# Slot sums of experts 0 to 3 over all 512 columns at once, and where the output tokens stand among the slot sums

## The chip, the core and the metric

The kernel runs on one core of a Trainium2 chip. The metric is the device time of one execution in microseconds (us). A core has a matrix engine (TensorE, PE in the profile, with its weight loads as PEld), a vector engine (VectorE, DVE), a scalar engine (ScalarE, ACT), GpSimd (POOL) and a sync engine (SyncE, SP) that in this kernel issues nearly all of the DMAs. Matrix products land in PSUM, and DVE or ACT copies them from there to SBUF.

## What is computed

```python
attn_out = _attn_ref(q, k, v)                       # windowed attention, 4 x 8 x 576 x 64
x = attn_out.transpose(0, 2, 1, 3).reshape(2304, 512)
x = (x @ w_a * (x @ w_b)) @ w_out                   # gated product, d_ff 1536
logits = x @ phi                                    # 2304 x 32: 8 experts, 4 slots each
d = softmax(logits, axis=0); c = softmax(logits, axis=1)
slot_input = (d.T @ x).reshape(8, 4, 512)
for e in range(8):
    slot_out[e] = maximum(slot_input[e] @ w1[e], 0) @ w2[e]   # w1: 512x1024, w2: 1024x512
out = c @ slot_out.reshape(32, 512)                 # 2304 x 512
```

All inputs and outputs are float32. The change touches only the last two lines: the product with `w2`, here called the slot sums, and the product with `c`, here called the tokens.

## The kernel before

Up to about 457 us the kernel works through attention, the gated product and the logits. Then come the eight experts, in two units: unit `u` = 0 has experts 0 to 3, unit 1 has experts 4 to 7. The slots of four experts lie side by side in the matrix engine, 32 columns each, so four matmuls (one for each expert) make one group.

- **Weights.** `w1` and `w2` come by DMA, on SP's queue, through a list of places in SBUF (`fetch`, `source`, line 782). The order of the loads is fixed: `w1`; then `w2` of experts 0 to 3 over all 512 columns, then of experts 4 and 5 over all 512 columns (keys `"r"`); then `w2` of experts 6 and 7 in halves of 256 columns (keys `"c"`), the left halves of both experts first and the right halves last. A place is loaded again when the products that read it are done. The last load is issued before the first output is.
- **Slot sums** (`slots_out`, line 1022). For a half `n` of the 512 columns and a unit `u`, eight groups (`m` = 0 to 7) of four matmuls of 256 columns add into one PSUM tile `ops`. The trace shows two records for each of these float32 matmuls.
- **Choice of slots** (`pick`, line 1029). DVE copies `ops` to SBUF as `o` (line 1072), and four small matmuls with the selection matrix `sel` add both units' slots into `so`.
- **`split`** (lines 1035 and 1036) copies `so` to `sor` on ACT and then subtracts on DVE; the tokens read `sor`.
- **Tokens** (`tokens_out`). For one of nine pairs of token tiles `j` and a half `n`: two matmuls into a PSUM bank `op` (line 1048; four banks take turns), a copy to SBUF `ob` (line 1053) by ACT when the running number is even and by DVE when it is odd, and one DMA of 256 KB to the output (line 1054) on SP's queue. There are 18 of these: nine for the left half, nine for the right.

In the last block (from line 1057) the order on PE is written by hand. It is: left half, unit 0, unit 1; choice; right half, unit 0, where the left half's tokens begin behind `m` = 4; right half, unit 1, with the other left tokens behind `m` = 0 to 4; choice; the nine right tokens. The order on DVE and ACT in this block comes from a scheduler, in before; each engine then works in the order it was given.

Of the kernel before, what the change touches and what calls it, by code (L numbers as in the profile page):

```python
# [11 lines left out]
F32 = mybir.dt.float32  # L12
# [9 lines left out]
P = 128  # L22
# [32 lines left out]
MANUAL = {mybir.EngineType.PE}  # L55
# [9 lines left out]
def swa_glu_softmoe_kernel(  # L65
# [13 lines left out]
    nc = tc.nc  # L79
    B, H, S, D = q.shape  # L80
    NT, DM = out.shape
# [4 lines left out]
    NTILE = NT // P  # L86
# [5 lines left out]
    MF = F2 // P  # L92
# [5 lines left out]
    N_EX1 = 4  # L98
    N_EX2 = 6
    WHOLE = 6  # L100
    EARLY = 4
    HALF = DM // 2

    dram = ctx.enter_context(tc.tile_pool(name="dram", bufs=1, space=bass.MemoryType.DRAM))
# [4 lines left out]
    p2 = ctx.enter_context(tc.tile_pool(name="p2", bufs=2))  # L109
# [3 lines left out]
    pools = {}  # L113

    ps_ab = ctx.enter_context(tc.tile_pool(name="ps_ab", bufs=1, space=PSUM))
    ps_s = ctx.enter_context(tc.tile_pool(name="ps_s", bufs=1, space=PSUM))
# [670 lines left out]
    def use(key):  # L787
        used.add(key)
        return exw[key]
# [32 lines left out]
    for t in range(NFIRST, NTILE):  # L822
        s = sA[t]
# [12 lines left out]
    for t in range(NTILE):  # L836
        if t < NTILE - NLAST:
            r = R[t]
# [7 lines left out]
            if t + 1 in beside:  # L846
                p = R[t + 1] - r
                o = (1, 2, 3) if p == 3 else (p / 3, 2 * p / 3, p)
            else:
                o = (1, 2.5, 3)  # L850
# [10 lines left out]
    a, b, c = LAST  # L861
# [83 lines left out]
    with tc.manual_schedule(engines=MANUAL | {mybir.EngineType.Activation, mybir.EngineType.DVE}):  # L945
# [8 lines left out]
        for m in range(MJ):  # L954
            for j in range(4):
                f = MJ * j + m
# [9 lines left out]
        for h in range(2):  # L966
            c = slice(DM // 2 * h, DM // 2 * (h + 1))
# [46 lines left out]
    def w2(e, m, n):  # L1014
        h, c = m // 4, m % 4
        if e >= WHOLE:
            return use(("c", (n, h, e), c))
        return (use if n else exw.get)(("r", (h, e), c))[:, HALF * n:HALF * n + HALF]

    def slots_out(op, u, m, n):  # L1020
        for e in range(4):
            nc.tensor.matmul(  # L1022
                op[32 * e:32 * e + 32], lhsT=hTs[u][m // 4][:, m % 4, 32 * e:32 * e + 32], rhs=w2(4 * u + e, m, n),
                start=(m == 0), stop=(m == MF - 1),
            )

    def pick(so, u, o):

        nc.tensor.matmul(
            so, lhsT=exs["sel"][:, u].rearrange("p a s -> p (a s)"), rhs=o, start=(u == 0), stop=(u == 1)  # L1030
        )

    def split(so):
        sor = exs["ex2"].tile([P, HALF], F32R, tag="as0", name="sor", bufs=2)
        nc.scalar.copy(out=sor, in_=so)
        nc.vector.tensor_tensor(out=sor[W:P], in0=so[W:P], in1=sor[W:P].bitcast(F32), op=ALU.subtract)
        return sor
# [5 lines left out]
    def tokens_out(n, j, sor):  # L1043
        i = j + NTILE // 2 * n
        pool, tag = banks[i % 4]
        op = pool.tile([P, 2, HALF], F32, tag=tag, name="op")
        for k in range(2):
            nc.tensor.matmul(op[:, k], lhsT=cts[2 * j + k], rhs=sor)  # L1048
        if i % 4 == 0:
            tag = ("w2", "w2", "w1", "w1", "w3")[i // 4]  # L1050
            obs[0] = wp.tile([P, 4, 2, HALF], F32, tag=tag, name="ob", bufs=wbufs[tag])
        ob = obs[0][:, i % 4]
        evac[i % 2](out=ob, in_=op)
        nc.sync.dma_start(
            out=out[2 * P * j:2 * P * (j + 1), HALF * n:HALF * (n + 1)].rearrange("(i p) d -> p i d", p=P), in_=ob
        )

    with tc.manual_schedule(engines=MANUAL):
        for n in range(2):
            os = {}  # L1060
            so = (ps_m, ps_t)[n].tile([P, HALF], F32, tag="mx"[n], name="so", bufs=1)
            for u in range(2):
                op = ps_s.tile([P, HALF], F32, tag=f"s{u}", name="ops")
                for m in range(MF):
                    slots_out(op, u, m, n)
                    if n and u and m < NTILE // 2 - EARLY:
                        tokens_out(0, EARLY + m, sor)
                    if n and not u and m >= MF - EARLY:
                        tokens_out(0, m - MF + EARLY, sor)
                for c in range(0, HALF, P):  # L1070
                    os[u, c] = p2.tile([P, P], F32, tag="l4", name="o", bufs=3)
                    nc.vector.tensor_copy(os[u, c], op[:, c:c + P])
                    for v in range(2 if u else 0):
                        pick(so[:, c:c + P], v, os[v, c])
            sor = split(so)
        for j in range(NTILE // 2):
            tokens_out(1, j, sor)


# [28 lines left out]
```

## Time and profile before

| | us |
|---|---|
| time, median of 3 runs (523.2 to 524.25) | 523.6 |
| the profiled execution | 524.17 |
| its span, first to last instruction | 522.4 |
| PE busy in the span | 489.7 (94%) |
| DVE, ACT, POOL busy | 297.6, 193.7, 65.5 |
| DMA moved | 116.51 MB, mean 223 GB/s |

The profiled execution is 524.17 - 522.4 = 1.77 us longer than its span. The busy shares are means over stages that have different limits. The change lies in the last 45 us of the span, and this stretch has three parts: weights arrive while the slot sums are formed (to 496 us), PE works without a gap of note (to 511 us), and the output drains (to 522.4 us). Times below are counted from the start of the span.

### The profile page before, as it was taken

Reading aid. Unit: us, or ns where it says so; the run is one execution under the profiler, and the core shown is the slowest. Engines: PE = TensorE matmul, PEld = TensorE weight load, DVE = VectorE, ACT = ScalarE, POOL = GpSimd, SP = SyncE. Lnnn points to the kernel's source line nnn. Section 1 sums busy time; section 2 is a strip of 40 time slices with the busy share of each in tenths; the row PEclk is TensorE's granted clock in tenths of the full one; section 3 lists DMA queues with packets and bytes.
Section 4 is the critical chain, followed back from the end, with each engine's and each line's share of the span. In section 5 each row is a group of like instructions: output and inputs, shape, how many; then the busy total and the mean of one; then the engine's idle time right before and its main releaser. Section 6 shows DMA issues by size and latency. Waiting matters only on the chain.

```text
span 522.4 us, 10689 instructions
## 1 busy us (share of the span) xinstructions
PE 489.7 (94%) x4047; PEld 361.7 (69%) x4047; DVE 297.6 (57%) x753; ACT 193.7 (37%) x586; POOL 65.5 (13%) x136
## 2 busy tenths in 40 slices
PE   5769999899999999999999999999999999999593
PEld 3547787678778787777777778787787777534252
DVE  3998898689146757647574755676833210512033
ACT  4786766544214423324232432343422112330022
POOL 4100100000000112120311112123331000100000
PEclk9798999999999999999999999999999999999798
DMA  9999965642136877678786776787799999799956
GB/s 254 271 274 295 311 166 203 220 142 80 42 77 155 205 203 202 187 177 206 202 199 173 157 187 166 175 217 187 197 246 315 337 356 335 263 404 396 355 180 204
DMA packets 135043, 116.51 MB, mean 223 GB/s; under 512 B 81744, under 2 KB 111952, under 8 KB 134992
## 3 DMA queue, kind: packets, MB, share of 16 engines
q1 hardware_dynamic: 130256, 101.15, 67.3%
q0 software_dynamic: 4736, 14.68, 9.6%
q8 instruction: 32, 0.52, 0.4%
q14 instruction: 19, 0.16, 0.1%
HBM read 91.16 MB, written 24.64 MB: 222 GB/s over the span
## 4 chain that ended last, share of the span: by engine, by line
PE 77%; DMA 11%; DVE 7%; ACT 2%; issue 1%; SPq 0%; DVEq 0%
PE psb L455 27%; PE psa L455 25%; DMA xw<-in_moe_w_dram 6%; PE xps L365 3%; DMA wo_dram<-wo 3%; PE s L274 3%; PE ups L633 3%; PE ops L1022 3%; PE ups L530 2%; PE tk L139 1%; PE op L1048 1%; PE tg L139 1%; PE tq L139 1%; PE tp L139 1%; PE two L139 1%
## 5 line engine op out<-in xcount | busy, mean ns | idle before, releaser
L455 PE MATMUL psb<-wb,x 128*128 128x512 f32 x648 | 167.1, 400 | 1.8 <-DVE g L467 1.4
L455 PE MATMUL psa<-wa,x 128*128 128x512 f32 x648 | 167.5, 400 | 0.0
L455 PEld LDWEIGHTS psb<-wb,x 128*128 128x128 f32 x648 | 117.4, 188 | 29.1 <-issue 2.8
L455 PEld LDWEIGHTS psa<-wa,x 128*128 128x128 f32 x648 | 117.5, 188 | 26.5 <-issue 3.2
L467 DVE TENSOR_TENSOR g<-psb,g 128x512 f32<-128x512 f32 (+1 forms) x54 | 36.6, 679 | 69.8 <-PE psb L455 61.6
L462 ACT COPY g<-psa 128x512 f32<-128x512 f32 x53 | 30.9, 583 | 84.0 <-PE psa L455 79.9
L294 ACT ACTIVATE pr<-pr,nmx 128x128 f32<-128x128 f32 x96 | 37.2, 389 | 17.6 <-DVE nmx L287 17.6
L331 POOL DMA_DIRECT2D pd<-pq x44 | 24.2, 559 | 101.7 <-DVE pq L324 72.6
L503 DVE STREAM_TRANSPOSE gq<-g 128x512 f32<-128x512 f32 x42 | 29.4, 703 | 0.7
L368 ACT CAST x<-xps 128x512 fp32r<-128x512 f32 x18 | 10.5, 585 | 47.5 <-PE xps L365 47.5
L1022 PE MATMUL ops<-xw,hT 128*32 128x256 f32 x256 | 19.9, 414 | 5.6 <-DMA xw<-in_moe_w_dram 5.6
L315 DVE TENSOR_TENSOR pr<-pr,rs 128x512 f32<-128x512 f32 x36 | 24.6, 689 | 1.0
L274 PE MATMUL s<-kTs,qTs 64*64 64x128 f32 x576 | 22.0, 294 | 0.0
L337 POOL DMA_DIRECT2D pT<-pd x22 | 16.5, 755 | 42.3 <-DMA pd<-pq 38.1
L274 PEld LDWEIGHTS s<-kTs,qTs 64*64 64x64 f32 x576 | 17.1, 144 | 5.9 <-issue 4.5
L237 POOL COPY kTs<-kTs 128x256 f32<-128x256 f32 x17 | 8.6, 503 | 97.6 <-DVE kTs L248 65.3
L139 PE MATMUL tq<-ident,ldq 128*128 128x128 f32 x72 | 12.4, 300 | 9.0 <-DMA ldq<-in_q_dram 7.6
L229 ACT ACTIVATE qTs<-tq 128x512 f32<-128x512 f32 x18 | 10.8, 599 | 26.5 <-PE tq L139 26.5
L287 DVE CUSTOM_DVE_ANT_0 pr<-s,masks 128x128 f32<-128x128 f32 x80 | 17.5, 284 | 3.1 <-PE s L274 3.1
L566 ACT ACTIVATE e<-lt,nm 128x128 f32<-128x128 f32 x17 | 6.2, 365 | 34.1 <-DVE nm L562 33.9
L294 ACT ACTIVATE pr<-s,nmx 128x128 f32<-128x128 f32 x48 | 17.0, 376 | 2.8 <-DVE nmx L284 2.8
L294 ACT ACTIVATION_READ_ACCUMULATOR pr<-pr,nmx 128x1 f32 x96 | 17.9, 187 | 0.0
(151 smaller groups left out, 612.5 us busy)
## 6 DMA issues: line engine op xcount, KB each, us to landing
xw<-in_moe_w_dram SPq DMA_DIRECT2D x42, 512.0 KB, 7.0
gd<-gq SPq DMA_DIRECT2D x168, 64.0 KB, 3.0
gT<-gd SPq DMA_DIRECT2D x42, 256.0 KB, 3.3
xw<-in_moe_w_dram SPq DMA_DIRECT2D x26, 256.0 KB, 7.9
st<-in_moe_w_b_dram SPq DMA_DIRECT2D x12, 512.0 KB, 5.7
st<-in_moe_w_out_dram SPq DMA_DIRECT2D x12, 512.0 KB, 5.2
st<-in_moe_w_a_dram SPq DMA_DIRECT2D x12, 512.0 KB, 7.0
pd<-pq POOLq DMA_DIRECT2D x44, 128.0 KB, 3.4
```

The source lines that it names most:

```text
L139: nc.tensor.transpose(o, i, ident)
L274: nc.tensor.matmul(sps[h][c, u], lhsT=qT[r, u, c], rhs=kTs[r, t % 2, u, W * b:W * b + P], start=not early, stop=not early or u == 3,)
L287: nc.vector.tensor_tensor_reduce(out=pr[:, u].rearrange("p (a k) -> p a k", a=2), in0=sps[h][:, u].rearrange("p (a k) -> p a k", a=2), in1 ...
L294: nc.scalar.activation(out=pr[:, u], in_=sps[h][:, u] if early else pr[:, u], func=ACTF.Exp, scale=-1.0, bias=nmx[:, i:i + 1], accum_out=s ...
L315: nc.vector.tensor_tensor(out=pr, in0=pr, in1=rs.to_broadcast([P, 4, P]), op=ALU.mult)
L331: nc.gpsimd.dma_start(out=pd[:, :, i].rearrange("j k e -> k j e"), in_=pq[32 * i:32 * i + 32].rearrange("p j h u q -> p j (h u q)"),)
L337: nc.gpsimd.dma_start(out=pT, in_=pd[:, :, :, P * h:P * h + P].rearrange("j k i e -> (j k) i e"))
L455: nc.tensor.matmul(ps, lhsT=l[:, kk], rhs=r, start=(n == 0), stop=(n == 3 * KD - 1))
L462: nc.scalar.copy(out=pas[t, fg], in_=ps)
L467: nc.vector.tensor_tensor(out=g[:, c:c + step], in0=ps[:, c:c + step], in1=pa[:, c:c + step], op=ALU.mult)
L503: nc.vector.transpose(out=gq.rearrange("p (j c t) -> p c j t", j=4, c=4), in_=gts[t][:, 512 * fg:512 * fg + 512].rearrange("p (c j f) -> p ...
L1022: nc.tensor.matmul(op[32 * e:32 * e + 32], lhsT=hTs[u][m // 4][:, m % 4, 32 * e:32 * e + 32], rhs=w2(4 * u + e, m, n), start=(m == 0), sto ...
```

## The change

The slot sums of unit 0 are formed once, over 512 columns (`slots_out` without `n`), instead of twice over 256; one DVE copy of 512 columns takes the place of four of 128. Unit 1 keeps its two halves. The left half's tokens no longer stand among the groups of the slot sums: five of them (`EARLY` = 5) stand between unit 1's left and right half, and the other four stand behind the choice of the right half, ahead of the nine right tokens. The order on ACT and DVE in this block is now the program's order too.

```diff
-    EARLY = 4
+    EARLY = 5
...
+        if n is None:
+            return use(("r", (h, e), c))
         return (use if n else exw.get)(("r", (h, e), c))[:, HALF * n:HALF * n + HALF]
 
-    def slots_out(op, u, m, n):
+    def slots_out(op, u, m, n=None):
...
-    with tc.manual_schedule(engines=MANUAL):
+    NOUT = NTILE // 2
+    sors = []
+    with tc.manual_schedule(engines=MANUAL | {mybir.EngineType.Activation, mybir.EngineType.DVE}):
+        op = ps_s.tile([P, DM], F32, tag="s0", name="ops")
+        for m in range(MF):
+            slots_out(op, 0, m)
+        o = pools["p3"].tile([P, DM], F32, tag="gT0", name="o", bufs=2)
+        nc.vector.tensor_copy(o, op)
         for n in range(2):
-            os = {}
+            op = ps_s.tile([P, HALF], F32, tag=f"s{1 - n}", name="ops")
+            for m in range(MF):
+                slots_out(op, 1, m, n)
             so = (ps_m, ps_t)[n].tile([P, HALF], F32, tag="mx"[n], name="so", bufs=1)
-            for u in range(2):
-                op = ps_s.tile([P, HALF], F32, tag=f"s{u}", name="ops")
-                for m in range(MF):
-                    slots_out(op, u, m, n)
-                    if n and u and m < NTILE // 2 - EARLY:
-                        tokens_out(0, EARLY + m, sor)
-                    if n and not u and m >= MF - EARLY:
-                        tokens_out(0, m - MF + EARLY, sor)
-                for c in range(0, HALF, P):
-                    os[u, c] = p2.tile([P, P], F32, tag="l4", name="o", bufs=3)
-                    nc.vector.tensor_copy(os[u, c], op[:, c:c + P])
-                    for v in range(2 if u else 0):
-                        pick(so[:, c:c + P], v, os[v, c])
+            for c in range(0, HALF, P):
+                o1 = p2.tile([P, P], F32, tag="l4", name="o", bufs=3)
+                nc.vector.tensor_copy(o1, op[:, c:c + P])
+                pick(so[:, c:c + P], 0, o[:, HALF * n + c:HALF * n + c + P])
+                pick(so[:, c:c + P], 1, o1)
             sor = split(so)
-        for j in range(NTILE // 2):
-            tokens_out(1, j, sor)
+            sors.append(sor)
+            for j in range(EARLY, NOUT) if n else ():
+                tokens_out(0, j, sors[0])
+            for j in range(NOUT if n else EARLY):
+                tokens_out(n, j, sor)
```

On PE, from the last transpose ahead of the slot sums to the end, the order before is this (rows that repeat are cut from the middle; `x63` are 63 matmuls in a row, `ops` are slot sums, `so` is the choice, `op` are tokens at two matmuls each):

```order
L139 MATMUL th<-ident,hs 128x128 x4
L1022 MATMUL ops<-xw,hT 32x256 x63
L1029 MATMUL so<-o,sel 128x128 x4
L1022 MATMUL ops<-xw,hT 32x256 x20
L1048 MATMUL op<-sor,cT 128x256 x2
...
L1022 MATMUL ops<-xw,hT 32x256 x12
L1029 MATMUL so<-o,sel 128x128 x4
L1048 MATMUL op<-sor,cT 128x256 x18
```

and now:

```order
L139 MATMUL th<-ident,hs 128x128 x4
L1024 MATMUL ops<-xw,hT 32x512 x31
L1024 MATMUL ops<-xw,hT 32x256 x32
L1031 MATMUL so<-o,sel 128x128 x4
L1050 MATMUL op<-sor,cT 128x256 x10
L1024 MATMUL ops<-xw,hT 32x256 x32
L1031 MATMUL so<-o,sel 128x128 x4
L1050 MATMUL op<-sor,cT 128x256 x26
```

Between the two choices there stood 64 matmuls of 256 columns and nine tokens; now there are 32 and five tokens, and 13 tokens stand behind the second choice where nine stood. The first 32 matmuls of unit 0 (one of them ahead of the transposes) are 512 columns wide.

On DVE, from the copies of the first slot sums to the end, before:

```order
L1072 COPY o<-ops 128x128 x4
L1036 TENSOR_TENSOR sor<-so,sor 64x256
L1053 COPY ob<-op 128x512
L1072 COPY o<-ops 128x128
L1053 COPY ob<-op 128x512
L1072 COPY o<-ops 128x128
L1053 COPY ob<-op 128x512 x2
L1072 COPY o<-ops 128x128 x2
L1036 TENSOR_TENSOR sor<-so,sor 64x256
L1053 COPY ob<-op 128x512 x5
```

and now:

```order
L1067 COPY o<-ops 128x512
L1075 COPY o<-ops 128x128 x2
L1038 TENSOR_TENSOR sor<-so,sor 64x256
L1055 COPY ob<-op 128x512 x2
L1075 COPY o<-ops 128x128 x2
L1038 TENSOR_TENSOR sor<-so,sor 64x256
L1055 COPY ob<-op 128x512 x7
```

Two output copies stand ahead of the second `sor` and seven behind it, where four and five stood. On ACT it is three and six, where it was five and four.

## Rows read from the trace of the kernel before

**Rows 1.** Chain that ended last: start us, us, what.

```profile
481.88 8.79 DMA xw<-in_moe_w_dram
...
490.71 5.17 PE ops L1022 x58
495.88 1.32 PE so L1029 x8
497.20 2.30 PE ops L1022 x40
...
507.95 1.43 PE ops L1022 x24
509.38 1.36 PE so L1029 x8
...
510.77 0.38 ACT sor L1035
...
511.17 0.44 DVE sor L1036
...
511.66 0.52 PE op L1048 x2
```

**Rows 2.** Timeline, slot sums: start us, us, engine, line, records [idle before <-releaser].

```profile
479.94 4.07 PE L1022 MATMUL ops<-xw,hT 128*32 128x256 f32 x66
488.46 1.06 PE L1022 MATMUL ops<-xw,hT 128*32 128x256 f32 x2 [4.45 <-DMA xw<-in_moe_w_dram]
493.73 1.66 PEld L1022 LDWEIGHTS ops<-xw,hT 128*32 128x32 f32 x26 [0.26 <-DMA xw<-in_moe_w_dram]
```

**Rows 3.** Timeline, unit 0 of the product with w1, 512 columns wide.

```profile
461.98 7.07 PE L989 MATMUL h<-xw,sinT 128*32 128x512 f32 x64 [0.38 <-DVE sinT L980]
```

**Rows 4.** Windows: stretch, its length, busy of each engine; last: PEclk, DMA share, GB/s.

```profile
13.00:14.00 1.00, 0.14 (x2) 0.00 (x0) 0.97 (x2) 1.00 (x5) 0.00 (x0) 1.00 0.99 387
15.00:16.00 1.00, 0.60 (x4) 0.42 (x4) 1.00 (x3) 1.00 (x2) 0.00 (x0) 0.99 0.99 296
16.00:17.00 1.00, 0.44 (x3) 0.45 (x3) 1.00 (x2) 1.00 (x6) 0.47 (x1) 0.50 1.05 324
483.00:484.00 1.00, 1.00 (x14) 0.34 (x6) 0.29 (x2) 0.00 (x0) 0.00 (x0) 1.00 1.05 422
487.00:488.00 1.00, 0.00 (x0) 0.00 (x0) 0.00 (x0) 0.00 (x0) 0.00 (x0) 0.51 1.10 347
490.70:493.80 3.10, 3.09 (x32) 1.45 (x36) 0.00 (x0) 0.00 (x0) 0.00 (x0) 0.50 1.10 348
504.00:505.00 1.00, 1.00 (x14) 0.45 (x14) 0.02 (x1) 0.56 (x1) 0.00 (x0) 1.00 0.66 227
```

**Rows 5.** Timeline, the first left token's copy and the right tokens behind the second choice.

```profile
499.96 0.59 ACT L1053 COPY ob<-op 128x512 f32<-128x512 f32 x1 [2.29 <-PE op L1048]
512.20 3.27 DVE L1053 COPY ob<-op 128x512 f32<-128x512 f32 x5 [0.59 <-PE op L1048]
512.92 2.71 SPq L1054 DMA_DIRECT2D out_dram<-ob  x5
```

**Rows 6.** Windows in the drain (columns as in rows 4).

```profile
511.00:512.00 1.00, 0.34 (x3) 0.34 (x3) 0.43 (x1) 0.14 (x1) 0.00 (x0) 1.00 0.04 12
514.00:515.00 1.00, 0.74 (x5) 0.37 (x3) 1.00 (x3) 0.89 (x2) 0.00 (x0) 1.00 1.03 337
519.00:520.00 1.00, 0.00 (x0) 0.00 (x0) 0.00 (x0) 0.00 (x0) 0.00 (x0) 0.50 1.01 339
521.00:522.40 1.40, 0.00 (x0) 0.00 (x0) 0.00 (x0) 0.00 (x0) 0.00 (x0) 0.50 0.00 0
```

**Rows 7.** DMA issues: line, queue, count, KB each, median us to landing.

```profile
out_dram<-ob SPq DMA_DIRECT2D x18, 256.0 KB, 2.6
```

## The prediction

> **What bounds the kernel now.** I read the end of the chain of waits first, since the change lies there alone; then the timeline of the same stretch; then windows of 1 us, for clock and DMA. The last 45 us fall into three parts with three limits.
>
> Up to 495.88 us the limit is the arrival of weights. Unit 0 and the first two matmuls of unit 1 are done at 479.94 + 4.07 = 484.01; then PE waits 4.45 us for expert 6, starts it at 488.46, waits again for expert 7 and goes on at 490.71 [rows 1, 2]. After the long wait the granted clock is 0.50 (1.2 GHz) from 487.0 on, and it is back at 1.00 (2.4 GHz) just after 493.8 [rows 4].
>
> From 495.88 to 511.66 the chain is PE alone: choice, 64 narrow matmuls with nine tokens among them, choice, `sor` [rows 1].
>
> From there the limit is the output. The first copy of a right token ends at 512.20 + 3.27/5, about 512.88, and its DMA is issued at 512.92 [rows 5]. Copies end at 515.47, the span only at 522.4. From 514 on the DMA share is 1.01 to 1.04 at 337 to 345 GB/s, seven us long [rows 6]. So the drain is a transfer of 9 x 262.1 KB = 2.36 MB; at 340 GB/s that is 6.94 us, 0.77 us a token. From 512.90 to 522.4 are 9.50 us; what is not transfer is 9.50 - 6.94 = 2.56 us (the first DMA's start, and the landing and end behind the last).
>
> **The change, part by part.**
>
> *Unit 0 over 512 columns.* The nearest row is the product with `w1`, also 128x32 by 512 columns: 64 records in 7.07 us, 0.110 us each [rows 3]; a narrow record is 4.07/66 = 0.062 [rows 2]. 64 records become 64 x 0.048 = 3.1 us longer, so PE reaches expert 6's first matmul at about 484.01 + 3.1 = 487.1 instead of 484.01. Expert 6 lands at 488.46, so the wait covers it with 1.35 us to spare, and expert 7's wait has 2.2 us more behind that. The loads themselves don't move: the last is issued ahead of the first output, and the places they wait for are freed by the product with `w1`. Price: 0, and 3.1 us if the cover were gone. The 512-wide DVE copy (one 512-wide output copy is 0.65 us [rows 5]) lies in the same wait.
>
> *The end of unit 1, left half.* PE now pauses 3.6 us, with one matmul in it, instead of 6.7 us. If the clock still falls, the end stays at 495.88. If it holds, the limit becomes the last left weight, for which a weight load last waited at 493.73 [rows 2]; 26 records from there at 0.058 are 1.5 us, so 495.2. Earlier in the trace the clock also fell at 16.0, after PE had stood from 13.14 until 15.4 and had worked 0.60 us in 15 to 16 [rows 4]; that is nearest to the new pause, so I take 495.88 and keep 495.2.
>
> *Between the choices.* Removed: 32 matmuls (64 records) and four of nine tokens. Left, from the end of the left sums:
> choice and `sor`: 511.66 - 509.38 = 2.28 us [rows 1]. In before, this `sor` was hidden behind right-half slot sums; now PE waits for it, since the tokens stand next in its queue.
> Five tokens: four find free banks, the fifth waits for the first copy. First pair of matmuls 0.52 [rows 1], ACT's copy 0.59 [rows 5], the fifth's own pair about 0.3: 1.4 us. The slot sums stand behind that wait, and behind them everyone. The lower end is five pairs without a wait, about 1.1, the upper one with two waits, 2.0; I take 1.45.
> 32 matmuls of unit 1, right half, all weights there by now: 64 records at 2.30/40 to 1.43/24 [rows 1], 3.7 to 3.8; I take 3.75.
> So the right sums end at 495.88 + 2.28 + 1.45 + 3.75 = 503.36; before, at 509.38. Gain here 6.02 us (5.5 to 6.3; 0.7 more if the clock holds).
>
> *The first copy of the drain.* Behind the second choice PE now has four left tokens that don't need the new `sor`; their matmuls run while ACT and DVE make it. DVE's subtraction ends 511.17 + 0.44 - 509.38 = 2.23 us after the right sums [rows 1], DVE's first output copy 0.7 later: 503.36 + 2.95 = 506.3. Before, 3.5 us lay between sums and first copy. Gain 0.55.
>
> *The drain.* 13 tokens instead of nine. DVE makes seven copies at 0.65 (4.6 us), ACT six beside it; the transfer needs 13 x 0.77 = 10.0 us, so it stays the limit. SP sends five in 2.71 us, 0.54 each [rows 5], also less than 0.77. The five early tokens are issued from about 499.3 on, 3.9 us of transfer, and are out by 504.5; their median landing is 2.6 us [rows 7]. End: 506.3 + 10.0 + 2.56 = 518.9. The drain costs 4 x 0.77 = 3.08 us more.
>
> Sum: 6.02 + 0.55 - 3.08 = 3.5 us off the span, 522.4 to 518.9. The profiled execution is 524.17, so its like would be 520.7; against the median of 523.6 the same 3.5 us give 520.1. With the clock held: 519.4.
>
> On the drain's rate the Trainium skill, "DMA: Bandwidth & Descriptors", section "Where 436 GB/s comes from", has two ceilings, about 435 GB/s for the fabric and about 358 for memory. The rows have 422 while weights are read [rows 4], over the lower one, and 337 to 345 while output is written, under both. At 358 a token would take 0.73 us and the drain 9.5, half a us less in the sum; I stay with the row's 0.77.
>
> **The rivals.**
>
> *A: the drain doesn't grow.* PE's last token would come about 5 us sooner, and if the writes overlapped better than now, the end would follow PE: 506.3 + 9.5 = 515.8, time 517.0. Against it: the drain's windows are full at a share of 1.01 to 1.04, so there is nothing left to overlap with. For it: from about 504.5 to 507 nothing is written in my sum, and were the fifth to eighth token issued sooner, that hole would close in part. Range 517.0 to 518.5.
>
> *B: the drain is slower than 0.77 a token.* 13 transfers wait for copies, for SP and for each other in one queue. In the interleaved stretch a token takes 1.00 us with DMA at 227 GB/s in the window 504 to 505 [rows 4]; at that rate 13 + 2.56 + 506.3 = 521.9, time 523.1, no change that can be told. Against it: there the pace is that of PE, which makes one token a us. Between, at 0.9, the time is 521.8.
>
> *C: slower, by the clock.* PE now stands at three places where it had work: for the first `sor` (0.9 us), for the bank of the fifth token, and, had the clock been low, with all of it at 1.2 GHz. Price at the low level: 32 records take 3.10 us at 0.50 [rows 4], so 64 take 6.2, 2.45 over 3.75; two choices at most 1.3 each, five tokens at most 0.5: at most 5.55 in all. The time is then 522.6 to 525.6, and it is slower than before beyond what can be told from 4.6 us on, that is, only if the clock stays low from 495 through the second choice. Against it: in 511 to 512 PE is busy 0.34, around it 0.73 and 0.93, and the clock stays 1.00 [rows 6]. The Trainium skill, "TensorE: Matmul & The Clock Gate", section "A second HAM failure mode: psum-queue depth-cycling", tells of this: PE idles briefly and often between groups that take PSUM banks in turn, and the clock swings between its levels. By that rule this rival's price is due; the trace of before shows the same bank turns at the end of the kernel without a fall.
>
> *D: the change doesn't do what it says.* The order on PE, DVE and ACT is the one described, so I give it nothing.
>
> **How the numbers follow.** The forecast, 519.4 to 520.1 with 0.6 us around it, has 0.76; A 0.07; B 0.10, half of it close to 523; C 0.07, most of it slower. A measurement of this kernel can tell about 0.2% (1.05 us) from no change. Faster by more: 0.76 + 0.07 + 0.05 = 0.88; within 0.2%: 0.05 + 0.02 = 0.07; slower: 0.05. The predicted time is the forecast's, 520.1. The range, 518.3 to 521.8, takes in both ends of the clock, the bounds of the tokens (0.5 to either side) and B up to 0.9 us a token; it leaves out most of A, the slow half of B, and C: 0.18.
>
> **What would show it.** In the profile of the changed kernel: unit 0's slot sums last about 7 us and still end ahead of 488.5; the left sums end at 495.2 to 495.9; a gap on PE of about 0.9 us ahead of the first token, with the release by DVE's `sor`; right sums end near 503.4; first copy behind the second choice ends near 506.3; then a DMA share of about 1.0 for 10 us, and the end near 518.9. Wrong would be: right sums that end later than 505 (C, or banks that hold PE), a drain window that is not full (B), or an end within 10 us of the first copy (A). If the drain's share is full but its rate is under 330 GB/s, the 0.77 was mis-sized.

## The result and the profile after

The changed kernel takes 520.06 us (median of nine runs, 516.86 to 521.91), the kernel before on the same occasions 524.34 us (nine runs, 523.2 to 526.25). The ratio is 0.9907, with a 95% interval of 0.9879 to 0.9935. The forecast was 520.1 in a range of 518.3 to 521.8, and a gain of 3.5 us; the medians differ by 4.3 us.

The profiled execution of the changed kernel happens to be the fastest of the nine: 516.86 us, with a span of 515.1. That is 7.3 us less than the profiled span of before, and not all of it is the change. So the traces are compared by distances between marks that both have, not by their ends. The marks are: the start of the product with `w1` (**start**), the wait for expert 7's first weights (**expert 7**), the end of the left slot sums (**left**), the end of the right slot sums (**right**) and the **end** of the span.

The timeline of PE after, to be read against [rows 1 to 3] (start us, us, engine, line, what, records, [idle before <-releaser]):

```profile
460.76 7.07 PE L989 MATMUL h<-xw,sinT 128*32 128x512 f32 x64 [0.38 <-DVE sinT L980]
479.16 7.49 PE L1024 MATMUL ops<-xw,hT 128*32 128x512 f32 x68
487.66 1.93 PE L1024 MATMUL ops<-xw,hT 128*32 128x256 f32 x32 [1.01 <-DMA xw<-in_moe_w_dram]
490.65 1.91 PE L1024 MATMUL ops<-xw,hT 128*32 128x256 f32 x26 [1.06 <-DMA xw<-in_moe_w_dram]
494.87 1.69 PE L1050 MATMUL op<-sor,cT 128*128 128x256 f32 x10 [0.98 <-DVE sor L1038]
496.48 3.66 PE L1024 MATMUL ops<-xw,hT 128*32 128x256 f32 x64
```

Unit 0 is one wide block. Counting records (two a matmul, 64 of unit 0 with the two that stand ahead of the transposes), the first 70 take PE past experts 4, 5 and 6 of the first group, so the wait at 487.66 is the one for expert 7's first load; the one at 490.65, with 26 records still to come, is for expert 7's **second load** of the left columns, which groups `m` = 4 to 7 read. For expert 6 PE doesn't wait here. In before, the wait at 488.46 was for expert 6 and the one at 490.71 for expert 7's first load [rows 1, 2].

The chain from there (start us, us, what), against [rows 1]:

```profile
490.65 1.91 PE ops L1024 x26
492.57 1.33 PE so L1031 x8
...
494.38 0.44 DVE sor L1038
494.82 0.04 issue
494.87 1.69 PE op L1050 x10
496.55 3.59 PE ops L1024 x64
500.14 1.36 PE so L1031 x8
501.51 0.02 issue
501.53 0.38 ACT sor L1037
```

and the windows (busy of each engine; last three: granted clock, DMA share, GB/s), against [rows 4, 6]:

```profile
486.00:488.00 2.00, 0.99 (x15) 0.37 (x14) 0.69 (x1) 0.00 (x0) 0.00 (x0) 1.00 1.10 348
490.00:492.00 2.00, 1.35 (x25) 0.81 (x26) 0.00 (x0) 0.00 (x0) 0.00 (x0) 1.00 1.10 349
503.00:504.00 1.00, 0.77 (x6) 0.80 (x7) 0.94 (x3) 0.09 (x2) 0.00 (x0) 1.00 0.48 156
504.00:506.00 2.00, 1.99 (x14) 1.56 (x13) 2.00 (x4) 1.83 (x4) 0.00 (x0) 1.00 1.03 342
512.00:513.00 1.00, 0.00 (x0) 0.00 (x0) 0.00 (x0) 0.00 (x0) 0.00 (x0) 0.50 1.01 345
513.00:514.00 1.00, 0.00 (x0) 0.00 (x0) 0.00 (x0) 0.00 (x0) 0.00 (x0) 0.50 0.50 174
```

The granted clock stays at 1.00 (2.4 GHz) through the waits for weights and to the end of PE's work. The DMA is full from about 503.5 to 513.5, ten us, and the span ends 1.6 us later.

Distances, in us, from the chains and timelines of all traces (the runs are described below):

| kernel | start to expert 7 | expert 7 to left | left to right | left to end |
|---|---|---|---|---|
| before | 28.73 | 5.17 | 13.50 | 26.5 |
| before again (e8) | 27.87 | 5.03 | 13.48 | 26.5 |
| cover only (e4) | 27.54 | 4.93 | 13.49 | 26.5 |
| tokens only (e5) | 27.46 | 6.44 | 10.11 | 25.0 |
| changed | 26.90 | 4.91 | 7.57 | 22.5 |
| changed again (e1) | 27.07 | 4.92 | 7.57 | 22.5 |
| narrow first (e10) | 28.24 | 4.93 | 7.58 | 22.6 |
| tokens among sums (e3) | 27.39 | 4.92 | 8.84 | 21.9 |
| eight early (e2) | 27.20 | 4.92 | 8.52 | 21.5 |
| two groups first (e7) | 27.63 | 4.93 | 7.64 | 20.6 |
| four unwritten (e6) | 27.08 | 4.93 | 7.57 | 21.7 |
| four more writes (e9) | 27.38 | 4.93 | 7.58 | 25.8 |

The last column is the change's own effect, 26.5 to 22.5; it repeats to 0.1 us between the two traces of before and between the two of the changed kernel. The first column, and the start itself (460.76 to 463.33 over these traces), differ from trace to trace by up to 1.8 and 2.6 us. That is of the size of the scatter between executions (516.86 to 521.91 for the changed kernel); that all of the scatter comes from there is not shown.

### The profile page after: what moved, and what is told of

Its sections match the earlier page's. It is cut to its first block, busy times and chain, and to the rows that moved or that the text cites. A ratio compares the mean times of both kernels' runs of the same rounds, so it can differ in the third digit from the quotient of the medians.

```text
span 515.1 us, 10557 instructions
## 1 busy us (share of the span) xinstructions
PE 485.1 (94%) x3983; PEld 359.4 (70%) x3983; DVE 296.8 (58%) x750; ACT 193.5 (38%) x586; POOL 65.4 (13%) x136
## 4 chain that ended last, share of the span: by engine, by line
PE 76%; DMA 12%; DVE 6%; ACT 2%; issue 1%; SPq 0%; DVEq 0%; ACTq 0%
PE psb L455 27%; PE psa L455 25%; DMA xw<-in_moe_w_dram 6%; PE xps L365 4%; PE s L274 3%; DMA wo_dram<-wo 3%; PE ups L633 3%; PE ups L530 2%; PE tq L139 2%; PE tk L139 1%; PE tg L139 1%; PE ops L1024 1%; PE tp L139 1%; PE two L139 1%; DMA ldk<-in_k_dram 1%
## 5 line engine op out<-in xcount | busy, mean ns | idle before, releaser
L455 PEld LDWEIGHTS psa<-wa,x 128*128 128x128 f32 x648 | 117.5, 188 | 26.5 <-issue 3.2
L229 ACT ACTIVATE qTs<-tq 128x512 f32<-128x512 f32 x18 | 10.8, 599 | 26.6 <-PE tq L139 26.5
L1024 PE MATMUL ops<-xw,hT 128*32 128x256 f32 (+1 forms) x192 | 16.0, 452 | 2.1 <-DMA xw<-in_moe_w_dram 2.1
```

What stands on the lines that cost most here:

```text
L455: nc.tensor.matmul(ps, lhsT=l[:, kk], rhs=r, start=(n == 0), stop=(n == 3 * KD - 1))
L1024: nc.tensor.matmul(op[32 * e:32 * e + 32], lhsT=hTs[u][m // 4][:, m % 4, 32 * e:32 * e + 32], rhs=w2(4 * u + e, m, n), start=(m == 0), sto ...
```

## The experiments

**Does the first trace repeat?**

> The changed kernel as it is, for a second trace. Theory of the prediction: the distances stay as in the first trace: 7.5 us from the end of the left slot sums to the end of the right ones, 15.0 us from there to the end of the span; what differs from run to run is the end of the left sums, which hangs on the arrival of the last left weights and on the clock (492.6 in the first trace, 495.9 forecast). Rival: the left sums end at the same time in each run and the drain's rate differs: then the distance from the right sums to the end varies by 2 us or more. A third: the runs differ ahead of the experts, in the first 460 us.

The median is 519.37 us (six runs, ratio 0.9912, 0.9889 to 0.9935). The chain:

```profile
492.17 1.91 PE ops L1024 x26
494.09 1.33 PE so L1031 x8
...
498.07 3.59 PE ops L1024 x64
501.66 1.36 PE so L1031 x8
```

Left to right is 7.57 us, and from there to the end of the span at 516.6 it is 14.9, as in the first trace. The left sums end 1.5 us later than in the first trace; of this, 1.34 us are already present when the product with `w1` starts (462.10 for 460.76). The expected forms "left sums differ" and "the first 460 us differ" both hold; a varying drain does not.

**The kernel before, again.**

> The kernel before as it is, for a second trace. Theory: 26.5 us from the end of the left sums to the end, as in the first trace; the start of the experts and the arrival of expert 7's first weights after it (28.7 us in the first trace, 26.9 to 27.5 in five others) differ from run to run by 1 to 2 us. Rival: 28.7 us belongs to the kernel before, so the changed kernel also makes the weights come sooner.

```profile
489.79 5.03 PE ops L1022 x58
494.82 1.32 PE so L1029 x8
```

The median is 524.16 us (eight runs) against 524.25. The span of the trace is 521.3, so left to end is 26.5 again. Expert 7 comes 27.87 us after the start, not 28.73. It is 27.54 and 27.46 in two more kernels that have unit 0's sums in the old order, and 26.9 to 28.2 in the eight traces with the hoist (unit 0 whole ahead of unit 1). The two sets overlap, so these traces don't show that the change makes the weights come sooner; some tenths of a us they couldn't tell.

**The pause and the clock.** The kernel before, with PE kept at work in the wait by 24 matmuls that nobody reads:

```diff
+                if not n and not u:
+                    dm = ps_t.tile([P, HALF], F32, tag="x", name="dm", bufs=1)
+                    for m in range(6):
+                        for e in range(4):
+                            nc.tensor.matmul(dm[32 * e:32 * e + 32], lhsT=..., rhs=w2(e, m, 0), ...)
```

> The kernel before with 24 more matmuls of 256 columns behind unit 0's left sums (six groups, into a bank that nobody reads): nothing is saved, PE only works 3 us longer before it waits for expert 6. Theory, the shorter pause keeps the clock at 1.00 and the left sums then end as soon as their weights are there: they end 0.6 to 3 us sooner than in before, and the whole is faster by as much. Rival, only the weights' arrival counts: no difference from before.

Timeline and chain of this run:

```profile
489.77 1.93 PE L1022 MATMUL ops<-xw,hT 128*32 128x256 f32 x32 [1.63 <-DMA xw<-in_moe_w_dram]
492.79 1.91 PE L1022 MATMUL ops<-xw,hT 128*32 128x256 f32 x26 [1.09 <-DMA xw<-in_moe_w_dram]
```

The median is 523.48 us (12 runs) against 523.43, ratio 0.9999 (0.9978 to 1.0019): no change that can be told. Yet the clock did stay up, as the two bursts show (32 records in 1.93 us; 3.10 at 0.50 [rows 4]). It gains little here, because at full clock PE waits another 1.09 us for expert 7's second load. From expert 7 to the left sums it takes 4.93 us, against 5.17 and 5.03 in the two traces of before. So the rival was right for the time: against these two traces of before, arrival sets the left sums, and the clock gave 0.1 to 0.24 us where 0.6 to 3 were expected.

**The tokens moved, without the hoisted unit 0.**

```diff
-                    if n and u and m < NTILE // 2 - EARLY:
-                        tokens_out(0, EARLY + m, sor)
-                    if n and not u and m >= MF - EARLY:
-                        tokens_out(0, m - MF + EARLY, sor)
+                for j in range(5) if n and u else ():
+                    tokens_out(0, j, sor)
...
+        for j in range(5, NTILE // 2):
+            tokens_out(0, j, left)
```

> The kernel before with the narrow halves of unit 0, but the tokens where the change has them: five ahead of the right half's unit 1, four behind the second choice. Theory: from the end of the left sums to the end of the right ones 1.3 + 3.75 + 1.5 + 3.75 = 10.3 us (before 13.5), drain 15.0 us from the right sums (before 13.0): 25.3 us in all against 26.5 before and 22.5 in the changed kernel. So 1.2 us faster than before; most of the gain is the wide unit 0. Rival: the place of the tokens carries the gain: 23.5 us or less.

The median is 522.16 us (ten runs, ratio 0.9965, 0.9942 to 0.9987), 2.1 below its before. Left to end is 25.0 us: 1.5 less than before, 2.5 more than the changed kernel. So the place of the tokens is the smaller part. ACT and DVE keep the scheduler's order in this kernel; from the right sums to the end it takes 14.9 us with 13 tokens, as in the changed kernel (14.95). So the program's order on ACT and DVE, which was not run alone, shows no share in the drain. This run also shows the clock at its dearest. Its chain, and windows around the wait:

```profile
488.25 6.44 PE ops L1022 x58
494.69 1.32 PE so L1029 x8
...
504.80 1.35 PE so L1029 x8
```

```profile
487.00:488.00 1.00, 0.00 (x0) 0.00 (x0) 0.00 (x0) 0.00 (x0) 0.00 (x0) 0.56 1.10 346
490.00:491.00 1.00, 1.00 (x16) 0.54 (x12) 0.00 (x0) 0.00 (x0) 0.00 (x0) 0.50 1.10 348
493.00:494.00 1.00, 1.00 (x16) 0.51 (x9) 0.00 (x0) 0.00 (x0) 0.00 (x0) 0.52 1.11 350
```

The clock falls at 487.1, and here it is back only just before 494, 5.7 us after PE went on; in the profiled run of before it was back after 3.1. With 6.44 us from expert 7 to the left sums instead of 4.93, the low clock costs 1.5 us. So in the three traces with a fall it cost between 0.1 and 1.5 us, the more, the longer the low level lasted after PE went on.

**The hoisted unit 0, with tokens among the sums.** Seven left tokens stand among unit 1's groups and two behind the second choice (before, all nine stood between the choices):

```diff
             for m in range(MF):
                 slots_out(op, 1, m, n)
+                if n and m:
+                    tokens_out(0, m - 1, sors[0])
...
-            for j in range(EARLY, NOUT) if n else ():
+            for j in range(MF - 1, NOUT) if n else ():
                 tokens_out(0, j, sors[0])
-            for j in range(NOUT if n else EARLY):
+            for j in range(NOUT if n else 0):
```

> The wide unit 0 alone: the left tokens stand among the right half's groups of unit 1 again, one behind each of m = 1 to 7, two behind the second choice; so 11 in the drain. Theory: the pause for the first choice vanishes, but each token costs PE 0.43 us among the sums: right sums end 8.7 us behind the left ones instead of 7.5, drain 2 x 0.77 = 1.54 shorter: 0.3 us faster than the changed kernel, so nearly all of the gain belongs to the wide unit 0. Rival: the gain comes from where the tokens stand: then it is 2 us or more slower than the changed kernel.

```profile
495.55 1.32 PE so L1031 x8
...
504.39 0.93 PE so L1031 x8
```

The median is 518.46 us (six runs, ratio 0.9895, 0.9867 to 0.9923). Left to end is 21.9 us (495.55 to 517.4), 0.6 less than the changed kernel: the hoist carries the gain with the tokens among the sums too, and the change's place for the tokens gives 0.6 us of it back. The two medians against their own befores (ratios 0.9895 and 0.9912) can't tell these kernels from each other; the distance can.

**Wide or narrow.**

```diff
-        for m in range(MF):
-            slots_out(op, 0, m)
+        for n in range(2):
+            for m in range(MF):
+                slots_out(op[:, HALF * n:HALF * n + HALF], 0, m, n)
```

> The changed kernel with unit 0 in two halves of 256 columns, one behind the other, both ahead of unit 1: the same place as in the change, without the wider matmuls. Theory, the gain comes from when unit 0 is worked and not from the width: 64 matmuls in about 7.9 us instead of 32 in 7.1, still hidden in the wait for expert 7, and 22.5 us from the end of the left sums to the end, as in the changed kernel. Rival, the width matters: the left sums end later behind expert 7's first weights than 4.9 us, or the whole is 1 us slower.

The median is 519.65 us (eight runs, ratio 0.9916, 0.9887 to 0.9944). The timeline:

```profile
480.58 7.53 PE L1024 MATMUL ops<-xw,hT 128*32 128x256 f32 x130
490.85 1.93 PE L1024 MATMUL ops<-xw,hT 128*32 128x256 f32 x32 [1.64 <-DMA xw<-in_moe_w_dram]
493.87 1.92 PE L1024 MATMUL ops<-xw,hT 128*32 128x256 f32 x26 [1.09 <-DMA xw<-in_moe_w_dram]
```

The block of 130 records holds 126 of unit 0's 128 and takes 7.53 us; the wide block holds 62 of 64, with six of unit 1, and took 7.49. Left to end is 22.6. What counts is that the right half of unit 0 is done while weights are awaited, not the width.

**Eight tokens between the choices instead of five.**

```diff
-    EARLY = 5
+    EARLY = 8
```

> Eight left tokens between the choices instead of five (EARLY = 8), so ten behind the second choice instead of 13. Theory, the end is set by 0.77 us of transfer a token: right sums 1.0 to 1.1 us later (three more tokens at about 0.35), drain 3 x 0.77 = 2.3 us shorter: 1.2 to 1.3 us faster than the changed kernel. Rival A of the prediction, the drain does not depend on the number of tokens: 1.0 us slower than the changed kernel.

```profile
493.68 1.33 PE so L1031 x8
...
502.20 1.36 PE so L1031 x8
```

Left to end is 21.5 us, 1.0 less than the changed kernel, where 1.2 to 1.3 was expected: the right sums end 0.95 us later and the drain is 1.95 shorter (13.0 from the right sums for 14.95). Three tokens at 0.77 are 2.3; the DMA share was only 0.51 to 0.64 from 504 to 507, so the queue had a hole in this kernel. The time itself, 519.01 us (seven runs, ratio 0.9911, 0.9874 to 0.9948), is not to be told from the changed kernel's.

**What a token costs in the drain.** First the transfers of four tokens were left out, with their matmuls and copies in place, so that this kernel leaves 1.05 MB of the output unwritten:

```diff
+        if not n and j >= EARLY:
+            return
         nc.sync.dma_start(
```

> The changed kernel without the four output transfers of the left tokens behind the second choice; their matmuls and copies stay. These rows of the output are left unwritten, so the kernel leaves out 1.05 MB of writes. Theory, the drain is 0.77 us of transfer a token: from the right sums to the end 15.0 - 3.1 = 11.9 us. Rival A of the prediction, the drain follows PE and the copies: no more than 1 us shorter.

The median is 517.61 us (four runs, ratio 0.9881, 0.9844 to 0.9917). From the right sums (502.91) to the end (517.0) it took 14.1 us, only 0.9 less than the changed kernel. By the letter of the expectation that is rival A. But the windows show another thing:

```profile
506.00:507.00 1.00, 1.00 (x8) 1.00 (x8) 0.93 (x2) 0.24 (x1) 0.00 (x0) 1.00 0.00 0
507.00:508.00 1.00, 0.98 (x8) 0.71 (x7) 1.00 (x3) 0.86 (x2) 0.00 (x0) 1.00 0.00 0
508.00:509.00 1.00, 1.00 (x6) 0.69 (x6) 1.00 (x2) 0.95 (x2) 0.00 (x0) 1.00 0.73 244
514.00:515.00 1.00, 0.00 (x0) 0.00 (x0) 0.00 (x0) 0.00 (x0) 0.00 (x0) 0.50 0.98 347
```

From 505 to 508 next to nothing is transferred: PE, DVE and ACT go through the four left tokens first, and the first right token, now the first to be written, is issued at 507.37, 4.46 us behind the right sums, against 2.47 us for the first write in the changed kernel. From 508.2 on the DMA is full for seven us, nine tokens at 0.77. So the edit put a late start in the place of four transfers; the expectation had overlooked it, and the run doesn't decide between the two. The next one adds transfers and leaves the start alone:

```diff
         nc.sync.dma_start(
             out=out[2 * P * j:2 * P * (j + 1), HALF * n:HALF * (n + 1)].rearrange("(i p) d -> p i d", p=P), in_=ob
         )
+        if not n and j >= EARLY:
+            spare = dram.tile([2 * P, HALF], F32, tag="spare", name="spare", bufs=4)
+            nc.sync.dma_start(out=spare.rearrange("(i p) d -> p i d", p=P), in_=ob)
```

> The changed kernel with each of the four left tokens behind the second choice written a second time, to a spare place in memory: four transfers of 256 KB more, no other work. Theory, 0.77 us of transfer a token with the DMA full: 22.5 + 3.1 = 25.6 us from the end of the left sums to the end, about 3.1 us slower than the changed kernel. Rival A, the drain follows PE and the copies: less than 1 us slower.

```profile
494.79 1.33 PE so L1031 x8
```

```profile
516.00:518.00 2.00, 0.00 (x0) 0.00 (x0) 0.00 (x0) 0.00 (x0) 0.00 (x0) 0.50 1.02 345
```

Left to end is 25.8 us (494.79 to 520.6) against 22.5, 3.3 us for four transfers, 0.82 each. At 516 to 518, 13.6 us and more behind the right sums (502.37), the DMA is still full; in the changed kernel it was done 13.4 us behind them. The median is 522.02 us (ten runs, ratio 0.9966, 0.9941 to 0.9991). Rival A falls: the drain's length goes with the number of transfers.

**Both together, and better.** The hoisted unit 0; two groups of the right half while the first choice is copied; then eight left tokens; then six groups:

```diff
-    EARLY = 5
+    EARLY = 8
...
             for m in range(MF):
+                if n and m == 2:
+                    for j in range(EARLY):
+                        tokens_out(0, j, sors[0])
                 slots_out(op, 1, m, n)
...
-            for j in range(NOUT if n else EARLY):
+            for j in range(NOUT if n else 0):
                 tokens_out(n, j, sor)
```

> The wide unit 0, and between the choices: two groups of unit 1's right half while the first choice is copied, then eight left tokens, then the other six groups; ten tokens behind the second choice. Theory: left to right sums 1.3 + 0.95 + 2.6 + 2.85 = 7.7 us, drain 2.5 + 7.7 + 2.56 = 12.8: 20.5 us in all against 22.5 in the changed kernel, about 2 us faster than it. If the drain didn't depend on the number of tokens, it would take 15.0 and the whole 22.7: no gain.

```profile
495.67 1.32 PE so L1031 x8
496.99 1.00 PE ops L1024 x16
497.99 2.60 PE op L1050 x16
500.58 2.73 PE ops L1024 x48
503.31 1.36 PE so L1031 x8
```

Left to right is 7.64 us with eight tokens in it, where the changed kernel needed 7.57 for five, since no pause for `sor` is left. Left to end is 20.6 us (495.67 to 516.3), 1.9 less than the changed kernel. The median is 516.66 us (six runs, 516.05 to 518.05), ratio 0.9863 (0.9833 to 0.9893): the lowest of all. Its interval and the changed kernel's (0.9879 to 0.9935) overlap, so the times alone don't part the two; the distances are 1.9 us apart where repeated traces agree to 0.1.

## Why the prediction was right, point by point

- **Where the bound lies.** Right. The three parts of the last 45 us stand in each trace, and the gain is made between the left sums and the end: 26.5 us before, 22.5 after. The forecast, counted the same way, was 518.9 - 495.88 = 23.0.
- **Unit 0 hidden in the wait.** Right. The wide block with six records of unit 1 ends at 486.65, 7.49 us long, and PE still waits 1.0 us for expert 7. In the second trace it waits 1.2 us.
- **The end of the left sums.** Here a term was mis-sized. I took 495.88, and 495.2 with the clock held. The first trace has 492.57. The clock held, in all eight traces of kernels with the hoist and in that with the cover. But the pause that I forecast, 3.6 us with one matmul in it, came out as 1.0 us; the longest such pause in a trace with the hoist was 2.7 us (488.11 to 490.85 in e10), so a pause of 3.6 us stays untested. From expert 7 to the left sums it takes 4.91 us instead of 5.17, so the clock is 0.26 of this, where I had 0.68; PE, at full clock, has to wait for expert 7's second load, 3.0 us behind the first. The other 3.05 us are expert 7's weights, there at 487.66 instead of 490.71: 1.22 us from an earlier start and 1.83 from a shorter way between. Both vary between traces of one and the same kernel (the start by 1.34 us from after to e1, the way by 0.86 from before to e8), so nothing here puts them down to the change. In another run of the narrow kind (e5) the fall cost 1.5 us, so its price was rightly left as a range, and the range was too narrow at the upper end.
- **Between the choices.** 7.48 forecast, 7.57 measured: choice and `sor` 2.30 (2.28), tokens 1.69 (1.45), sums 3.59 (3.75). The pause of 0.98 us for DVE's `sor` stands ahead of the tokens, as said.
- **The first copy of the drain.** Wrong by 0.5 us. I had the first write follow DVE's copy of token 5, 2.95 us behind the right sums. SP's row of the first tail write stands at 502.61, 2.47 behind them, at the end of an ACT copy (the last row is PE's, in the same stretch):

```profile
502.00 1.07 ACT L1055 COPY ob<-op 128x512 f32<-128x512 f32 x2
502.39 4.61 DVE L1055 COPY ob<-op 128x512 f32<-128x512 f32 x7
502.61 8.83 SPq L1056 DMA_DIRECT2D out_dram<-ob  x13
503.23 3.04 PE L1050 MATMUL op<-sor,cT 128*128 128x256 f32 x18 [0.80 <-DVE ob L1055]
```

DVE's copy of token 5 starts at 502.39 and, at some 0.65 us, ends about 503.05, 2.9 us behind the right sums, as I had it. But ACT is free after its part of `sor` and has copied token 6 by then, and the write at 502.61, ahead of the end of DVE's copy, can only be that one. SP's order is not written by hand in this block. The step that failed is that I took the order of the writes from the order of the tokens and looked at the queues of PE, DVE and ACT alone.
- **The drain.** 12.56 us from first write to end forecast (10.0 and 2.56), 12.49 measured. 0.77 us a token held in the changed kernel; the test with four more transfers gave 0.82.
- **The sum.** 23.0 forecast from left to end, 22.5 measured; the missing 0.5 is the first copy. That the median is 0.04 us from the forecast is luck: the median of before moved up by 0.7 us with more runs, and the gain was 4.3, not 3.5.
- **The rivals.** A (drain doesn't grow) falls by e9. B (more than 0.77 a token) had 0.10; nothing like the 0.9 to 1.0 it needs was seen. C (clock falls behind the left sums): the clock is 1.00 from there to the end of PE's work. The rule of the Trainium skill, "TensorE: Matmul & The Clock Gate", section "A second HAM failure mode: psum-queue depth-cycling", would have made this rival come true. Here PE idles 0.98 us for `sor` and 0.80 for a bank in the tail, and the trace shows no fall.

The change gives 4.0 us from left to end. The hoisted unit 0 with seven tokens among the sums gives 4.6 (e3), the moved tokens alone 1.5 (e5). Both together, in the change's form, give less than e3: there the right sums end 1.27 us later behind the left ones (8.84 for 7.57), but 11 tokens instead of 13 are left behind them, and the drain is 1.9 us shorter (13.0 for 14.95).

## What to carry to other kernels

When an engine waits for data and later has work whose data is already there, move that work into the wait; its width matters little, its place does. When the end is a queue of transfers that runs full, count what is still to be sent from the moment of the first write, and move writes ahead of the last computation until the queue has no hole. Compare traces by distances between marks inside the part that was changed: executions that differ by several us (516.86 to 521.91 in one kernel) hide differences that two traces show to 0.1 us.

## What the runs showed that was not expected

The price of a clock fall went with how long the low level lasted after PE went on, not with the length of the pause. Three traces with unhoisted sums had pauses before expert 7 of 6.7, 5.8 and 5.4 us (before, e8, e5), each with expert 6's one matmul in it. After them the low level lasted 3.1, 2.8 and 5.7 us more, and the way from expert 7 to the left sums took 5.17, 5.03 and 6.44 us, against 4.91 to 4.93 without a fall: the shortest pause was the dearest. The 32 records up to expert 7's second load take 3.10 us at the low level; at the full one they take 1.93, and PE then waits 1.06 to 1.09 for that load. So the low level costs next to nothing up to there, and what lasts beyond it is paid. Why the level came back sooner or later these three traces don't show. Where unit 0 was hoisted, PE's waits there were two or three of 0.5 to 1.6 us with work between them, and the clock never fell.

Loads and writes ran at nearly the same rate where their pieces were equally short. Writes of 256 KB, 13 in a row, kept the DMA at 336 to 347 GB/s. The last loads of weights ran at 347 to 350 GB/s, those just before them at 405 (476 to 480 us) and 392 (480 to 484):

```profile
480.00:484.00 4.00, 4.00 (x44) 1.26 (x40) 0.00 (x0) 0.00 (x0) 0.00 (x0) 1.00 1.03 392
484.00:486.00 2.00, 2.00 (x24) 0.55 (x18) 0.00 (x0) 0.00 (x0) 0.00 (x0) 1.00 1.09 353
```

In this trace the packets of the loads are of 2048 and 6144 bytes up to 482 us and, from 484 on, of 1024 bytes, as the weights of experts 6 and 7 come in halves of 256 columns; the packets of the writes are of 1024 bytes too. So the 422 GB/s of loads beside the 337 to 345 of writes, as the prediction sets them, can't be put down to reading and writing: [rows 4] has loads at 347 and 348 as well. That the packets' size sets the rate fits both, but no run here changes it alone.
